# MoE2's gates of the second half and their sums kept in PSUM for VectorE, with low parts of the first half and of one tile of sums done by GpSimd

## The chip, the cores and the metric

The kernel runs on one core of a Trainium2 chip. The metric is the device time of one execution in microseconds (us), lower is better. The core has TensorE (PE; its weight loads are shown as PEld), VectorE (DVE), ScalarE (ACT), GpSimd (POOL) and SyncE (SP), which issues most of the loads and stores; each works through its own instructions in order and waits on semaphores for the others.

## The reference

```python
# q, k, v: (4, 8, 576, 64); 2304 tokens, model width 512
x = attention(q, k, v)          # softmax within chunks of 64 positions, 8 heads
p = domain_probs / sum(domain_probs)
y = sum(p[:, e] * (relu(x @ w1[e]) @ w2[e]) for e in range(4))     # MoE1, width 1024 for each e
h = y @ w_in                                                       # MoE2, (2304, 2048)
g = h * clip(h + 3, 0, 6) / 6                                      # the gates
out = g @ w_out                                                    # (2304, 512)
```

All is float32. The change concerns the last two lines.

## The kernel before

The 2304 tokens are worked on in three sets of 768. The program first runs MoE1 over the three sets (with the attention beside it), then MoE2 over the three sets; in MoE2 the width 2048 is cut into four groups of 512 (`g` = 0 to 3). One set and one group is a unit, so MoE2 has twelve units.

**Numbers.** Each float32 operand of TensorE is split into a high part (a rounded copy, made by ScalarE) and a low part (operand minus high part). A product is three matmuls: high by high, high by low, low by high (`HL`). `parts` makes the pair for gates and sums of gates: ScalarE writes the high part, then one TENSOR_TENSOR of VectorE or GpSimd writes the low part. TensorE's third matmul of each three needs the low part.

**The h part of a unit** (`h_pair`, two pairs, `pr_` = 0 and 1). Each pair is seven block products P1, P6, P7, P5, P2, P4, P3 of six matmuls of 384 columns, in four PSUM banks of tag `h` that are called a, b, c, d, with VectorE's additions `U`, `V`, `c22`, `c21`, `c12` between them (a Strassen form in Winograd's variant). `BACK` says where VectorE puts the results c22, c21, c12 of a pair: `p` in their own bank, `y` in a bank of tag `y`, `s` in SBUF. `gate` turns each of the four results of a pair into a gate: ScalarE's ACTIVATE makes the clipped part in an SBUF tile `t`, and VectorE's SCALAR_TENSOR_TENSOR (STT) multiplies it with the result in PSUM.

**The y part** (`y_sevens`, in the groups 0 to 2, nine units in all). The gates of a unit are four blocks A11, A12, A21, A22 of two tiles each (`k` = 0, 1; a tile is 128 x 384). Pair 0 gives A11 and A21, pair 1 gives A12 and A22. `gate_sums` makes S3 = A11 - A21, S1 = A21 + A22, S2 = S1 - A11 and S4 = A12 - S2, two tiles of each. TensorE then runs seven products in the order M1 (A11), M7 (S3), M2 (A12), M4 (A22), M5 (S1), M6 (S2), M3 (S4), each of 18 matmuls of 256 columns: three output tiles `j`, for each the six matmuls of `k` = 0 and then `k` = 1. M1 and M7, M2 and M4, M5 and M6 share banks, whose tags are in `YB`. In group 0 ScalarE copies the banks to totals in SBUF, in the groups 1 and 2 VectorE adds them (L1121). After group 2 `recombine` adds the totals to the output's blocks (L1135, two thirds on VectorE, a third on GpSimd). Group 3 is done plainly (`y_unit`, L1160, its additions L1203).

**PSUM** has eight banks here: four of tag `h`, three of `y`, one of `a`.

**GpSimd** also issues the loads of the split weights from scratch memory, in line with its additions: `wh` (L808, for the h part), `wy`, `wp` (L813) and `e` (L818, for the y part).

**The order.** All operations are handed to a planner (`Plan`) with an engine, an estimated cost (`dve`, `act`, `gps`, `mm`), a due time and what they need; it plays the program through with these costs and writes out a fixed order for each engine. So a new cost or due time can reorder an engine anywhere. `SLACK` and `LATER` are such numbers.

In the kernel before, all results of pair 1 are gated into SBUF tiles; the low parts of A11, A12, A22, S1 and S2 are VectorE's, those of S3 and S4 GpSimd's (`SLO`), and all sums are GpSimd's (L1056).

Of the kernel before, what the change touches and what calls it, by code (L numbers as in the profile page):

```python
# [22 lines left out]
SLACK = (7.93, 5.2, 6.37, 0.92)  # L23
# [218 lines left out]
def fused_kernel(ctx: ExitStack, tc: tile.TileContext, q, k, v, probs, w1, w2, win, wout, out):  # L242
# [80 lines left out]
    gps = lambda n: 0.03 + n * 0.0024  # L323
# [685 lines left out]
    def gate(u, f, z, src, bufs, after, due, n=N):  # L1009
# [9 lines left out]
        elif ph == 0:  # L1019
            hi = op("ACT", act(n), lambda: nc.scalar.activation(hi_(), src(), AF.Relu), due, after, [G], bufs)  # L1020
            lo = op("DVE", dve(n), lambda: nc.vector.scalar_tensor_tensor(out=lo_(), in0=src(), scalar=0.0, in1=raw(hi_()), op0=ALU.max, op1=ALU.subtract), due + 0.3, [hi, *after], (), [G, *bufs])  # L1021
        else:
            R = buf("t")
            r_ = lambda: R.t[:, :n]
            x = op("ACT", act(n), lambda: nc.scalar.activation(r_(), src(), AF.Relu, bias=half, scale=1.0 / 6.0), due, after, [R], bufs)  # L1025
            x = op("DVE", dve(n), lambda: nc.vector.scalar_tensor_tensor(out=r_(), in0=r_(), scalar=1.0, in1=src(), op0=ALU.min, op1=ALU.mult), due + 0.3, [x, *after], (), [R, *bufs])  # L1026
            if by_seven(u):
                name, k = A_OF[z, f % 2], f // 2
                raws[u, name, k] = (R, x)
                if name != "A21":  # L1030
# [55 lines left out]
    def y_sevens(u):  # L1086
# [6 lines left out]
        for q_, pair in enumerate(Y_PAIRS):  # L1093
            ps = [buf(YB[q_]) for _ in range(NJ)]
# [292 lines left out]
```

## Time and profile before

| | |
|---|---|
| median of 3 executions | 1214.36 us (1212.03 to 1214.58) |
| the profiled execution, and the span of its trace | 1214.51 us, 1212.7 us |
| busy: PE, DVE, POOL, ACT | 1176.5, 803.8, 675.9, 510.2 us |
| mean granted clock of TensorE | 0.994 |
| MoE2's first product starts at, span ends at | 815.28, 1212.7 us |

The span runs from the first to the last instruction; the remaining 1.8 us lie around it. Busy time is how long an engine had an instruction in it. Matmuls are pipelined and overlap in the trace, so the time that TensorE takes for a stretch of work is read from start to start, and the stalls from the idle time that the trace puts ahead of an instruction. The granted clock is 1.00 at 2.4 GHz and 0.50 at 1.2 GHz.

### The profile page before, as it was taken

The page shows a single profiled execution, that of the slowest core. Times are in us where ns is not written, and L with a number is a line of the kernel's source. Part 1 is how long each engine was busy: PE and PEld are TensorE (multiplying, and loading weights), DVE is VectorE, ACT ScalarE, POOL GpSimd, SP SyncE. Part 2 cuts the span into 40 slices and gives each one's busy share as a digit, 9 for nine tenths or more (in the row PEclk, how much of TensorE's full clock was granted, in tenths as well). Part 3 has the DMA queues.
Part 4 walks back from the last instruction along what each step waited for, and adds up shares of the span by engine and source line. Part 5 has one row for each costly group of instructions (what it writes and reads, how often), then busy time and mean ns, then how long its engine had stood idle before and what let it go on. Part 6 is the DMA issues. An engine that isn't in the chain of part 4 may idle for free.

```text
span 1212.7 us, 20698 instructions
## 1 busy us (share of the span) xinstructions
PE 1176.5 (97%) x7512; PEld 1077.7 (89%) x7512; DVE 803.8 (66%) x1414; ACT 510.2 (42%) x1205; POOL 675.9 (56%) x755
## 2 busy tenths in 40 slices
PE   8999999999999999999999999999999999899988
PEld 7898998888888999998998988989998999889987
DVE  5656555547466766567456566686889768976895
ACT  5755444433435343533332423245334453335322
POOL 3686665641464564737474756556663566526670
PEclk9999999999999999999999999999999999999999
DMA  9889877758789998777888988999965977577751
GB/s 241 290 305 321 276 263 252 277 202 265 213 261 316 279 334 265 261 245 246 266 287 277 323 254 274 351 295 257 303 218 194 262 256 236 169 239 243 229 171 53
DMA packets 153958, 311.27 MB, mean 257 GB/s; under 512 B 70528, under 2 KB 76928, under 8 KB 153856
## 3 DMA queue, kind: packets, MB, share of 16 engines
q0 software_dynamic: 48672, 172.51, 43.9%
q1 hardware_dynamic: 103440, 135.73, 34.9%
q10 hardware_dynamic: 1744, 1.70, 0.5%
q8 instruction: 59, 0.97, 0.3%
q14 instruction: 43, 0.35, 0.1%
HBM read 228.10 MB, written 81.79 MB: 256 GB/s over the span
## 4 chain that ended last, share of the span: by engine, by line
PE 81%; DVE 15%; ACT 2%; issue 2%; POOL 0%; DVEq 0%; POOLq 0%; ACTq 0%
PE h L937 37%; PE y L1160 33%; DVE gt L1050 4%; PE h L996 4%; PE y L1106 3%; DVE acc L1121 1%; DVE acc L1135 1%; DVE rh L1050 1%; PE h L1106 1%; DVE t L1026 1%; DVE xs L672 1%; DVE h L947 1%; DVE gt L1018 1%; DVE c L947 1%; PE a L545 1%
## 5 line engine op out<-in xcount | busy, mean ns | idle before, releaser
L937 PE MATMUL h<-x,wh 128*128 128x384 f32 x2772 | 494.1, 336 | 5.4 <-DVE c L947 5.2
L937 PEld LDWEIGHTS h<-x,wh 128*128 128x128 f32 x2772 | 482.0, 188 | 10.9 <-DVE c L947 7.8
L1160 PE MATMUL y<-wy,gt 128*128 128x512 f32 x1944 | 457.3, 393 | 4.7 <-DVE acc L1196 3.5
L1160 PEld LDWEIGHTS y<-wy,gt 128*128 128x128 f32 x1944 | 363.0, 188 | 82.5 <-DVE acc L1196 5.2
L808 POOL DMA_DIRECT2D wh<-k x190 | 104.7, 552 | 172.3 <-PE h L937 148.9
L1196 DVE SCALAR_TENSOR_TENSOR acc<-y,pn,acc 128x512 f32<-128x512 f32 x126 | 88.9, 750 | 129.9 <-PE y L1160 129.9
L813 POOL DMA_DIRECT2D wy<-k x112 | 61.9, 556 | 98.4 <-PE y L1160 84.6
L1020 ACT ACTIVATE gt<-h 128x384 fp32r<-128x384 f32 (+1 forms) x133 | 60.7, 484 | 112.4 <-DVE h L947 78.0
L1021 DVE SCALAR_TENSOR_TENSOR gt<-h,gt 128x384 fp32r<-128x384 f32 (+1 forms) x133 | 68.5, 539 | 43.3 <-ACT gt L1020 42.9
L947 DVE TENSOR_TENSOR c<-h,p 128x384 f32<-128x384 f32 x66 | 36.6, 555 | 85.1 <-PE h L937 70.5
L954 ACT COPY p<-h 128x384 f32<-128x384 f32 x66 | 31.4, 476 | 138.8 <-PE h L937 138.8
L1050 DVE TENSOR_TENSOR gt<-t,gt 128x384 fp32r<-128x384 f32 x96 | 86.5, 936 | 1.7 <-ACT gt L1048 0.5
L1056 POOL TENSOR_TENSOR t<-t 128x384 f32<-128x384 f32 x72 | 80.8, 1133 | 6.6 <-DVE gt L1050 4.9
L947 DVE TENSOR_TENSOR c<-h,c 128x384 f32<-128x384 f32 x120 | 66.4, 554 | 25.8 <-PE h L937 23.0
L1048 ACT CAST gt<-t 128x384 fp32r<-128x384 f32 x114 | 55.1, 513 | 55.6 <-POOL t L1056 28.7
L947 DVE TENSOR_TENSOR h<-h,c 128x384 f32<-128x384 f32 x111 | 62.5, 563 | 23.4 <-PE h L937 21.3
L873 POOL TENSOR_TENSOR w<-w,rh 128x512 f32<-128x512 f32 x28 | 37.4, 1336 | 52.4 <-issue 16.0
L728 POOL TENSOR_TENSOR wy<-t,wy 128x512 fp32r<-128x512 f32 x32 | 41.1, 1291 | 40.9 <-ACT wy L726 39.1
L1025 ACT ACTIVATE t<-h,half 128x384 f32<-128x384 f32 x72 | 39.6, 578 | 50.8 <-DVE h L947 38.3
L996 PE MATMUL h<-x,wh 128*128 128x384 f32 (+1 forms) x336 | 53.2, 314 | 0.5 <-DVE x L702 0.5
L996 PEld LDWEIGHTS h<-x,wh 128*128 128x128 f32 x336 | 51.4, 189 | 1.2 <-DVE x L702 0.7
L728 POOL TENSOR_TENSOR wp<-t,wp 128x512 fp32r<-128x512 f32 x32 | 43.8, 1368 | 13.4 <-ACT wp L726 13.0
(188 smaller groups left out, 1557.8 us busy)
## 6 DMA issues: line engine op xcount, KB each, us to landing
wh<-k POOLq DMA_DIRECT2D x190, 512.0 KB, 6.2
wy<-k POOLq DMA_DIRECT2D x112, 512.0 KB, 6.0
k<-wh SPq DMA_DIRECT2D x53, 512.0 KB, 3.7
k<-wp SPq DMA_DIRECT2D x53, 512.0 KB, 5.8
k<-wy SPq DMA_DIRECT2D x32, 512.0 KB, 3.2
wp<-k POOLq DMA_DIRECT2D x18, 512.0 KB, 5.8
t<-in_moe_w_dram SPq DMA_DIRECT2D x32, 256.0 KB, 4.7
w<-in_moe_w_in_dram SPq DMA_DIRECT2D x16, 512.0 KB, 6.0
```

What stands on the lines that cost most here:

```text
L728: return op(eng, gps(512) if eng == "POOL" else dve(512), lambda: e.tensor_tensor(out=view(b.t[:, 1]), in0=read(), in1=raw(view(b.t[:, 0]) ...
L808: wready[at_] = op("POOL", 0.6, lambda b=b, name=name: nc.gpsimd.dma_start(out=b.t, in_=kept[ph, g, name]), t - LEAD[0] + j, [stored[ph, g ...
L813: wready[key, "y", f] = op("POOL", 0.6, lambda b=b, f=f: nc.gpsimd.dma_start(out=b.t, in_=kept[ph, g, f]), t_y - LEAD[3] + n_, [stored[ph, ...
L937: nc.tensor.matmul(acc.t[:, :n], W.t[:, a, k_ * 256 + pr_ * P:k_ * 256 + (pr_ + 1) * P], X.t[:, b, k_, cs], start=new and first, stop=last ...
L947: add = lambda out, x, y: (lambda: nc.vector.tensor_tensor(out=out(), in0=x(), in1=y(), op=ALU.add))
L996: nc.tensor.matmul(ps.t[:, :m], Ws[k_ // 2].t[:, a, k_ % 2 * 256 + f % 2 * P:k_ % 2 * 256 + f % 2 * P + P], x if len(zs) == 2 else x[:, zs ...
L1020: hi = op("ACT", act(n), lambda: nc.scalar.activation(hi_(), src(), AF.Relu), due, after, [G], bufs)
L1021: lo = op("DVE", dve(n), lambda: nc.vector.scalar_tensor_tensor(out=lo_(), in0=src(), scalar=0.0, in1=raw(hi_()), op0=ALU.max, op1=ALU.sub ...
L1050: lo = op(eng, dve(N) if eng == "DVE" else gps(N), lambda: e.tensor_tensor(out=where()[:, 1], in0=r_(), in1=raw(where()[:, 0]), op=ALU.sub ...
L1056: return op("POOL", gps(N), lambda: nc.gpsimd.tensor_tensor(out=dst.t[:, :N], in0=x.t[:, :N], in1=y.t[:, :N], op=op_), due + m, after, new ...
L1160: nc.tensor.matmul(ps[j].t, G.t[:, a, o + j * P:o + (j + 1) * P], W.t[:, b, :], start=f == FO[0] and i == 0, stop=f == FO[-1] and i == len ...
L1196: fn = lambda: nc.vector.scalar_tensor_tensor(out=A.t, in0=ps.t, scalar=p, in1=A.t, op0=ALU.mult, op1=ALU.add)
```

## The change

Three tiles of pair 1 (`STAY`: both of A12, and `k` = 0 of A22) are gated in place: the STT writes to the PSUM bank of the result and not to the SBUF tile. Result c12 of pair 0 also stays in its own bank (`BACK`). What reads a gate in PSUM is VectorE's: the low parts of these three tiles, the sums S1, S2 of `k` = 0 and S4 of both `k`, the low parts of S1 and S4 of `k` = 0 (S1 of `k` = 0 is made in A22's bank, S4 of `k` = 0 in A12's, `S4_STAY`). GpSimd makes the low parts of A11 (both), A22 of `k` = 1, S1 of `k` = 1, S2 (both), S3 (both), S4 of `k` = 1, and the sums S3 (both), S1 and S2 of `k` = 1. Sums of `k` = 1 come first. `YB` now names a bank tag for each `j`. In a unit VectorE's low parts go from 10 to 5 and its sums from 0 to 4; GpSimd's low parts go from 4 to 9 and its sums from 8 to 4. TensorE's and ScalarE's instructions are as many as before.

```diff
-SLACK = (7.93, 5.2, 6.37, 0.92)
+SLACK = (7.97, 5.41, 6.27, 0.96)
...
-BACK = (("pys", "pps"), ("pys", "ppp"))
-SLO = ("DVE", "POOL", "DVE", "POOL")
+BACK = (("pys", "pps"), ("pyp", "ppp"))
 CO = ("DVE", "POOL", "DVE")
+STAY = (("A12", 0), ("A12", 1), ("A22", 0))
+S4_STAY = (0,)
 SUMS = 3.15
-YB = "yhyy"
-LATER = 0.35
+YB = ("yyy", "ahy", "yhh", "ahh")
+LATER = -1.0
...
-    gps = lambda n: 0.03 + n * 0.0024
+    gps = lambda n: 0.07 + n * 0.0024
...
             R = buf("t")
             r_ = lambda: R.t[:, :n]
+            name, k = (A_OF[z, f % 2], f // 2) if by_seven(u) else ("", 0)
+            stay = (name, k) in STAY
+            o_ = src if stay else r_
             x = op("ACT", act(n), lambda: nc.scalar.activation(r_(), src(), AF.Relu, bias=half, scale=1.0 / 6.0), due, after, [R], bufs)
-            x = op("DVE", dve(n), lambda: nc.vector.scalar_tensor_tensor(out=r_(), in0=r_(), scalar=1.0, in1=src(), op0=ALU.min, op1=ALU.mult), due + 0.3, [x, *after], (), [R, *bufs])
-            if by_seven(u):
-                name, k = A_OF[z, f % 2], f // 2
-                raws[u, name, k] = (R, x)
+            x = op("DVE", dve(n), lambda: nc.vector.scalar_tensor_tensor(out=o_(), in0=r_(), scalar=1.0, in1=src(), op0=ALU.min, op1=ALU.mult), due + 0.3, [x, *after], (), [R, *bufs])
+            if name:
+                raws[u, name, k] = (bufs[0] if stay else R, x)
                 if name != "A21":
-                    sevens[u, name, k] = parts("gt", R, [x], due + 0.6)
+                    sevens[u, name, k] = parts("gt", bufs[0] if stay else R, [x], due + 0.6, "DVE" if stay else "POOL")
+                rooms[u, name, k] = R
...
-        def sum_(dst, x, op_, y, after, m, new=()):
-            return op("POOL", gps(N), lambda: nc.gpsimd.tensor_tensor(out=dst.t[:, :N], in0=x.t[:, :N], in1=y.t[:, :N], op=op_), due + m, after, new, list({id(b): b for b in (dst, x, y)}.values()))
+        def sum_(eng, dst, x, op_, y, after, m, new=()):
+            e = nc.vector if eng == "DVE" else nc.gpsimd
+            return op(eng, dve(N) if eng == "DVE" else gps(N), lambda: e.tensor_tensor(out=dst.t[:, :N], in0=x.t[:, :N], in1=y.t[:, :N], op=op_), due + m, after, new, list({id(b): b for b in (dst, x, y)}.values()))
 
         def both(name, k, R, x, m):
             i = ("S1", "S3", "S2", "S4").index(name)
             tag = ("gt", "gt", "rh", "w64")[i]
-            share = (sevens[u, name, 0][0], 1) if tag == "rh" and k else None
-            sevens[u, name, k] = parts(tag, R, [x, *([sevens[u, name, 0][1]] if share else [])], due + m, SLO[i], share)
+            first = sevens.get((u, name, 1 - k))
+            share = (first[0], 1) if tag == "rh" and first else None
+            sevens[u, name, k] = parts(tag, R, [x, *([first[1]] if share else [])], due + m, "DVE" if name == "S1" and ("A22", k) in STAY or name == "S4" and k in S4_STAY else "POOL", share)
 
         if (u, "A22", 0) not in raws:
             for k in range(2):
                 (r11, x11), (r21, x21) = raws[u, "A11", k], raws[u, "A21", k]
                 s3 = buf("t")
-                both("S3", k, s3, sum_(s3, r11, ALU.subtract, r21, [x11, x21], 0, [s3]), 0.6)
+                both("S3", k, s3, sum_("POOL", s3, r11, ALU.subtract, r21, [x11, x21], 0, [s3]), 0.6)
             return
-        for k in range(2):
+        for k in (1, 0):
             (r11, x11), (r12, x12), (r21, x21), (r22, x22) = (raws[u, name, k] for name in ("A11", "A12", "A21", "A22"))
-            los = {name: sevens[u, name, k][1] for name in ("A11", "A12", "A22")}
-            s1 = sum_(r21, r21, ALU.add, r22, [x21, x22, sevens[u, "S3", k][1]], 0.1 * k)
-            both("S1", k, r21, s1, 0.8)
-            s2 = sum_(r11, r21, ALU.subtract, r11, [s1, los["A11"]], 2 + 0.1 * k)
-            both("S2", k, r11, s2, 2.8)
-            s4 = sum_(r12, r12, ALU.subtract, r11, [x12, s2, los["A12"]], 4 + 0.1 * k)
-            both("S4", k, r12, s4, 4.8)
-
-    sevens, raws, totals = {}, {}, {}
+            los = {name: sevens[u, name, k][1] for name in ("A11", "A22", "S3")}
+            m = 0.1 * (1 - k)
+            at = "DVE" if ("A22", k) in STAY else "POOL"
+
+            s1 = sum_(at, r22, r22, ALU.add, r21, [x21, x22, los["A22"]], m)
+            both("S1", k, r22, s1, 0.8 + m)
+            s2 = sum_(at, r11, r22, ALU.subtract, r11, [s1, los["A11"], los["S3"]], 1.2 + m)
+            both("S2", k, r11, s2, 2 + m)
+            R = r12 if k in S4_STAY else rooms[u, "A12", k]
+            s4 = sum_("DVE" if ("A12", k) in STAY else "POOL", R, r12, ALU.subtract, r11, [x12, s2], 3 + m)
+            both("S4", k, R, s4, 4 + m)
+
...
-            ps = [buf(YB[q_]) for _ in range(NJ)]
+            ps = [buf(YB[q_][j]) for j in range(NJ)]
```

**VectorE in the y part** of the second MoE2 unit (group 1 of the first set). `gt_`, `rh_`, `w64_` are high and low parts, `t_` SBUF tiles, `h_`, `y_`, `a_` PSUM banks, L1050 low parts, L1026 the STT, L1121 additions to totals. Before:

```order
L1026 SCALAR_TENSOR_TENSOR t_9449<-t_9449,h_9379 128x384
L1050 TENSOR_TENSOR gt_9470<-t_9439,gt_9470 128x384
L1050 TENSOR_TENSOR gt_9474<-t_9449,gt_9474 128x384
L1121 TENSOR_TENSOR acc_9111<-y_9430,acc_9111 128x512
L1121 TENSOR_TENSOR acc_9121<-y_9442,acc_9121 128x512
L1050 TENSOR_TENSOR gt_9500<-t_9348,gt_9500 128x384
L1050 TENSOR_TENSOR gt_9503<-t_9321,gt_9503 128x384
L1121 TENSOR_TENSOR acc_9143<-y_9454,acc_9143 128x512
L1050 TENSOR_TENSOR rh_9531<-t_9323,rh_9531 128x384
L1121 TENSOR_TENSOR acc_9173<-h_9493,acc_9173 128x512
L1121 TENSOR_TENSOR acc_9199<-h_9505,acc_9199 128x512
L1050 TENSOR_TENSOR rh_9531<-t_9345,rh_9531 128x384
```

In the change L1030 is the STT, L1054 low parts, L1061 sums, L1131 additions to totals:

```order
L1054 TENSOR_TENSOR gt_9436<-h_9337,gt_9436 128x384
L1030 SCALAR_TENSOR_TENSOR h_9376<-t_9447,h_9376 128x384
L1054 TENSOR_TENSOR gt_9457<-h_9365,gt_9457 128x384
L1131 TENSOR_TENSOR acc_9102<-y_9425,acc_9102 128x512
L1054 TENSOR_TENSOR gt_9469<-h_9376,gt_9469 128x384
L1131 TENSOR_TENSOR acc_9113<-y_9438,acc_9113 128x512
L1061 TENSOR_TENSOR h_9376<-h_9376,t_9348 128x384
L1131 TENSOR_TENSOR acc_9136<-y_9450,acc_9136 128x512
L1061 TENSOR_TENSOR t_9323<-h_9376,t_9323 128x384
L1061 TENSOR_TENSOR t_9432<-h_9365,t_9345 128x384
L1054 TENSOR_TENSOR gt_9518<-h_9376,gt_9518 128x384
L1061 TENSOR_TENSOR h_9337<-h_9337,t_9323 128x384
```

The rows with two SBUF tiles as inputs (`t_` with `gt_` or `rh_`) are gone: every row of the change reads a PSUM bank. Both low parts of S2 (`rh_`) have left VectorE, four sums have come, and the additions to totals now stand between them.

**GpSimd in the same y part**, from the low parts of S3 on. Before (L1056 sums, L1050 low parts, DMA rows are issues of loads):

```order
L1050 TENSOR_TENSOR gt_9390<-t_9376,gt_9390 128x384
L1050 TENSOR_TENSOR gt_9401<-t_9365,gt_9401 128x384
L808 DMA wh_9426<-k117_205 128x1024
L1056 TENSOR_TENSOR t_9321<-t_9321,t_9410 128x384
L808 DMA wh_9452<-k118_206 128x1024
L1056 TENSOR_TENSOR t_9345<-t_9321,t_9345 128x384
L808 DMA wh_9472<-k119_207 128x1024
L1056 TENSOR_TENSOR t_9348<-t_9348,t_9449 128x384
L1056 TENSOR_TENSOR t_9439<-t_9439,t_9345 128x384
L1056 TENSOR_TENSOR t_9323<-t_9348,t_9323 128x384
L813 DMA wy_9522<-k120_208 128x1024
L1056 TENSOR_TENSOR t_9412<-t_9412,t_9323 128x384
```

In the change (L1061 sums, L1054 low parts):

```order
L1054 TENSOR_TENSOR gt_9410<-t_9372,gt_9410 128x384
L1054 TENSOR_TENSOR gt_9422<-t_9403,gt_9422 128x384
L809 DMA wh_9460<-k117_205 128x1024
L1061 TENSOR_TENSOR t_9403<-t_9403,t_9321 128x384
L809 DMA wh_9485<-k118_206 128x1024
L1061 TENSOR_TENSOR t_9345<-t_9403,t_9345 128x384
L1054 TENSOR_TENSOR gt_9488<-t_9403,gt_9488 128x384
L809 DMA wh_9521<-k119_207 128x1024
L1054 TENSOR_TENSOR rh_9509<-t_9345,rh_9509 128x384
L814 DMA wy_9541<-k120_208 128x1024
L1054 TENSOR_TENSOR w64_9538<-t_9432,w64_9538 128x384
L1054 TENSOR_TENSOR rh_9509<-t_9323,rh_9509 128x384
```

Two sums (S1 and S2 of `k` = 1) stand where six did, and low parts of A22, S1 and S2 have come in; the low part of S2 of `k` = 0 (`rh_` from `t_9323`) is the last. The issues of loads are the same ones.

**VectorE in MoE1**, at the end of the second set's stretch, ahead of three additions L1196 to totals (L1206 in the change). Before:

```order
L702 TENSOR_TENSOR x7_65<-xs_4246,x7_65 128x768
L1018 TENSOR_TENSOR gt_6460<-c_6396,gt_6460 128x384
L870 TENSOR_SCALAR rh_6174<-t_6401 128x512
L702 TENSOR_TENSOR x7_65<-xs_4246,x7_65 128x768 x2
L672 TENSOR_TENSOR xs_4246<-xs_4246 128x2x384
L1196 SCALAR_TENSOR_TENSOR acc_3931<-y_6436,pn_79,acc_3931 128x512
L1196 SCALAR_TENSOR_TENSOR acc_3936<-y_6444,pn_79,acc_3936 128x512
L1196 SCALAR_TENSOR_TENSOR acc_3947<-y_6449,pn_79,acc_3947 128x512
```

In the change:

```order
L871 TENSOR_SCALAR rh_6174<-t_6401 128x512
L703 TENSOR_TENSOR x7_65<-xs_4246,x7_65 128x768
L1019 TENSOR_TENSOR gt_6463<-c_6396,gt_6463 128x384
L703 TENSOR_TENSOR x7_65<-xs_4246,x7_65 128x768
L673 TENSOR_TENSOR xs_4246<-xs_4246 128x2x384
L1206 SCALAR_TENSOR_TENSOR acc_3931<-y_6435,pn_79,acc_3931 128x512
L1206 SCALAR_TENSOR_TENSOR acc_3937<-y_6441,pn_79,acc_3937 128x512
L1206 SCALAR_TENSOR_TENSOR acc_3947<-y_6446,pn_79,acc_3947 128x512
```

Of the four wide operations on `xs` and `x7` (L702 and L672, in the change L703 and L673) that stand in these rows ahead of the additions, three are left; one L702 stands earlier in the list, and an L672 that stood there has moved behind the additions.

## Rows read from the trace of the kernel before

**Rows 1.** Waits of PE, 815 to 1213: who waited for whom, total, times, longest.

```profile
PE y L1106 <- DVE rh L1050: 10.9, 6, 2.2
PE h L937 <- DVE c L947: 5.2, 4, 1.9
PE h L1106 <- DVE gt L1050: 4.9, 8, 0.6
```

**Rows 2.** Timeline of PE in MoE2: start, us, instructions, idle before and its releaser.

```profile
815.28 12.67 PE L937 MATMUL h<-x,wh 128*128 128x384 f32 x72
...
830.96 4.47 PE L1106 MATMUL y<-wy,gt 128*128 128x256 f32 x36
...
840.30 2.30 PE L1106 MATMUL y<-wp,gt 128*128 128x256 f32 x18
...
846.76 14.72 PE L937 MATMUL h<-x,wh 128*128 128x384 f32 x84
861.32 4.47 PE L1106 MATMUL y<-wy,gt 128*128 128x256 f32 x36
...
913.28 5.37 PE L937 MATMUL h<-x,wh 128*128 128x384 f32 x30
...
929.88 8.36 PE L1160 MATMUL y<-wy,gt 128*128 128x512 f32 x36
...
946.73 14.75 PE L937 MATMUL h<-x,wh 128*128 128x384 f32 x84
...
1043.03 5.40 PE L937 MATMUL h<-x,wh 128*128 128x384 f32 x30
...
1061.86 8.36 PE L1160 MATMUL y<-wy,gt 128*128 128x512 f32 x36
...
1078.93 14.75 PE L937 MATMUL h<-x,wh 128*128 128x384 f32 x84
...
1176.18 5.37 PE L937 MATMUL h<-x,wh 128*128 128x384 f32 x30
...
1192.47 16.52 PE L1160 MATMUL y<-wy,gt 128*128 128x512 f32 x72
```

**Rows 3.** Timeline of DVE around the y part that starts at 861.32.

```profile
854.71 0.55 DVE L1050 TENSOR_TENSOR gt<-t,gt 128x384 fp32r<-128x384 f32 x1
...
859.88 1.09 DVE L1026 SCALAR_TENSOR_TENSOR t<-t,h 128x384 f32<-128x384 f32 x2 [0.92 <-ACT t L1025]
...
864.88 2.56 DVE L1050 TENSOR_TENSOR gt<-t,gt 128x384 fp32r<-128x384 f32 x2
```

**Rows 4.** Timeline of POOL in the same stretch.

```profile
856.08 2.33 POOL L1056 TENSOR_TENSOR t<-t 128x384 f32<-128x384 f32 x2
...
859.46 2.00 POOL L1050 TENSOR_TENSOR gt<-t,gt 128x384 fp32r<-128x384 f32 x2
```

**Rows 5.** Groups by line and shape, 815 to 1213: count, busy us, mean ns, idle before.

```profile
L1050 DVE TENSOR_TENSOR gt<-t,gt 128x384 fp32r<-128x384 f32 x96 | 86.5, 936 | 1.7 <-ACT gt L1048 0.5
L1056 POOL TENSOR_TENSOR t<-t 128x384 f32<-128x384 f32 x72 | 80.8, 1133 | 6.6 <-DVE gt L1050 4.9 <-DVE t L1026 0.9
...
L808 POOL DMA_DIRECT2D wh<-k x76 | 41.8, 551 | 86.0 <-PE h L937 86.0
...
L947 DVE TENSOR_TENSOR h<-h,c 128x384 f32<-128x384 f32 x48 | 27.1, 564 | 8.8 <-PE h L937 7.6
...
L1121 DVE TENSOR_TENSOR acc<-h,acc 128x512 f32<-128x512 f32 x18 | 11.7, 678 | 0.0
...
L672 DVE TENSOR_TENSOR xs<-xs 128x768 f32<-128x768 f32 x8 | 7.6, 955 | 0.0
```

**Rows 6.** Windows: busy us (count) of PE, PEld, DVE, ACT, POOL, granted clock, DMA.

```profile
908.50:911.90 3.40, 3.40 (x18) 3.40 (x18) 3.35 (x9) 0.00 (x0) 1.33 (x2) 0.50 0.70 231
1051.90:1055.20 3.30, 3.30 (x12) 3.30 (x11) 2.62 (x6) 2.02 (x4) 0.00 (x0) 0.50 0.00 0
```

**Rows 7.** Timeline of PE in MoE1: its longest stall there.

```profile
552.50 3.83 PE L1160 MATMUL y<-wy,gt 128*128 128x512 f32 x10 [1.83 <-DVE acc L1196]
```

More of the change, by code (lines that the diff above doesn't have):

```diff
@@ L1067, in gate_sums @@
                 s3 = buf("t")
-                both("S3", k, s3, sum_(s3, r11, ALU.subtract, r21, [x11, x21], 0, [s3]), 0.6)
+                both("S3", k, s3, sum_("POOL", s3, r11, ALU.subtract, r21, [x11, x21], 0, [s3]), 0.6)
             return
-        for k in range(2):
+        for k in (1, 0):
             (r11, x11), (r12, x12), (r21, x21), (r22, x22) = (raws[u, name, k] for name in ("A11", "A12", "A21", "A22"))
-            los = {name: sevens[u, name, k][1] for name in ("A11", "A12", "A22")}
-            s1 = sum_(r21, r21, ALU.add, r22, [x21, x22, sevens[u, "S3", k][1]], 0.1 * k)
-            both("S1", k, r21, s1, 0.8)
-            s2 = sum_(r11, r21, ALU.subtract, r11, [s1, los["A11"]], 2 + 0.1 * k)
-            both("S2", k, r11, s2, 2.8)
-            s4 = sum_(r12, r12, ALU.subtract, r11, [x12, s2, los["A12"]], 4 + 0.1 * k)
-            both("S4", k, r12, s4, 4.8)
-    sevens, raws, totals = {}, {}, {}
+            los = {name: sevens[u, name, k][1] for name in ("A11", "A22", "S3")}
[8 more added lines that the diff above has]
+            both("S4", k, R, s4, 4 + m)
+    sevens, raws, rooms, totals = {}, {}, {}, {}
     A_OF = {(0, 0): "A11", (0, 1): "A12", (1, 0): "A21", (1, 1): "A22"}
```

## The prediction

> **What bounds the kernel now.** TensorE is busy nearly everywhere, so what can be won is the time in which it stands. I read the views in this order: TensorE's waits, its timeline from start to start, the timelines of VectorE and GpSimd around one y part, then the groups by shape for prices. In MoE2, TensorE's waits are for VectorE alone [rows 1]: 10.9 us in 6 stalls for low parts of S2 (`rh`), 4.9 us in 8 for low parts of A12 (L1106 in `h` banks is M2), and 5.2 us for `c`, the sums U and V of an h part.
>
> The timeline gives the full loss [rows 2]. A clean h part takes 861.32 - 846.76 = 14.56 us. M5, M6 and M3 of the first unit ran clean: 54 matmuls in 846.76 - 840.30 = 6.46 us, 0.1196 us each, so a clean y part of 126 takes 15.07. From 830.96 to 1192.47 are 361.51 us. Taken off: eight clean h parts (116.48), the three h parts of the groups 3 (16.60 from 913.28, 18.83 from 1043.03, 16.29 from 1176.18: 51.72) and two plain y parts (929.88 to 946.73 and 1061.86 to 1078.93: 33.92). That leaves 159.39 us for nine y parts that need 135.6: **23.8 us lost**, 2.6 in each. Of it 10.9 + 4.9 are stalls. The rest is their aftermath, refilling and low clock: right after one of the longest stalls on S2, TensorE ran 3.4 us at a granted clock of 0.50, the level of 1.2 GHz [rows 6], which costs half of it, 1.7 us.
>
> Why VectorE is late stands in its timeline. A low part from two SBUF tiles takes 0.55 us alone (854.71) but two of them 2.56 at 864.88 [rows 3], while GpSimd was making sums; the mean over MoE2 is 0.936 [rows 5]. An STT that reads one SBUF tile and one PSUM bank kept 0.55 at 859.88 [rows 3] beside GpSimd's low parts, which kept 1.00 each from 859.46 [rows 4]. So two SBUF inputs meet GpSimd, and a PSUM input does not.
>
> **The change, walked through one y part.** T is the start of M1. Products start at T + 2.15 (M7), 4.31 (M2), 6.46 (M4), 8.61 (M5), 10.76 (M6) and 12.92 (M3); each needs the low part of `k` = 0 at its third matmul, 0.24 us later, and of `k` = 1 at its sixth.
>
> VectorE: c12 of pair 1 ends at about T + 0.8 in both kernels (TensorE's P3 ends at T + 0.2, plus 0.56). From there the order runs STT, low, STT, low, addition, low, addition, S1, addition, S2, S4, low of S1, S4. The trace has no row of these exact forms; between an STT's 0.55 and 0.564 for an addition into a bank [rows 5] I take 0.56, with 0.68 for additions to totals [rows 5]. Low parts of A12 are then ready by T + 3.1 (needed from 4.55, the second at 4.9), of A22 `k` = 0 by 4.3 (needed at 6.7), S1's by T + 0.8 + 9 x 0.56 + 3 x 0.68 = 7.9 (needed at 8.85), S4's by about 10.4 (needed at 13.2). S4 of `k` = 1, in the middle of this, needs GpSimd's S2, which by the next paragraph's prices is there at 4.9. So the A12 stalls go and no new one comes on this engine.
>
> GpSimd is now the long chain. Its second sum of S3 ended at 858.41 before [rows 4], T - 2.9; two low parts of A11 now stand ahead of it, one in time that was idle, so I take T - 2.4. Behind it come nine operations (two lows of S3, low of A22, S1, S2, low of S1, low of S2, low of S4, low of S2) and six issues of loads. At 1.03 (the pair's 1.00 [rows 4] and a little for starts after a pause) and 0.55 for an issue [rows 5], that is 9 x 1.03 + 6 x 0.55 = 12.6: the last low part lands at T + 10.2, and M6 needs it at 11.0. **Margin 0.8 us.** The first two must be there for M7 at 2.4: T - 2.4 + 2 x 0.55 + 2 x 1.03 = 0.8. The prices' other bound is 1.133, GpSimd's mean for sums while VectorE met it [rows 5]: then T + 11.1, and M6 waits 0.1. The loads behind need no early issue: they are for the next unit, 15 us on.
>
> The Trainium skill speaks against this part: "GPSIMD Engine Reference", section 4.1 "Engine selection", gives elementwise work on a tile to VectorE, with GpSimd about twice as slow for two inputs. The rows agree on the ratio (1.03 to 0.55). By the rule alone, five more low parts of 0.48 extra in nine units would add 21.6 us; by the rows they cost VectorE 0.94 in company and lie on neither engine's end, so the sum takes nothing for them.
>
> So the nine y parts give back **23.8 us**; bounds: 9.4, with a stall of 1.6 us in each (the first rival), and no more than all.
>
> The h part of the first unit lost 830.96 - 815.28 - 14.56 = 1.1 us [rows 2], the fourth of the stalls on `c`, where V stood behind three transposes on VectorE; in the new order one stands ahead of V: **-1.1**, bound 0.
>
> The h parts of the groups 3 lost 2.0, 4.3 and 1.7 us [rows 2], 8.0 in all, to `c` behind `recombine`, whose work is the same. Before, stalls in M6 gave VectorE time; now M6 and M3 run through, but VectorE no longer comes to its additions of M6 from a late low part of S2. I take a stall of 1.6 us, a little under the 1.9 of the second set [rows 1], and 0.15 for refilling in each, and the 1.7 of low clock once, as it came after that 1.9 [rows 6]: 5.2 + 1.7 = 6.9, so **-1.1**; bounds -2.8 (no low clock) and +2.3 (three times).
>
> MoE1 is reordered in small swaps. TensorE's longest stall there is 1.83 us at 552.50 [rows 7], for totals behind wide subtractions. One of these (0.955, [rows 5]) no longer stands ahead: **-1.0**. Bounds: the stall and its low clock gone, -3.5, or one more like it, +3.5.
>
> Sum: 23.8 + 1.1 + 1.1 + 1.0 = 27.0, from the profiled execution's 1214.5 (the median of the runs is 0.15 less): **1187.5 us**.
>
> **The rivals.**
>
> *GpSimd ends last.* Its chain has 0.8 us of margin. If VectorE's new forms still met it, an operation would take 1.16, the mean of the two sums at 856.08, or 1.30, what one of them took if the other took 1.03 [rows 4]. At 1.30 the chain ends 9 x 0.27 = 2.4 later, M6 stalls 1.6 in each y part, and 14.4 us stay: 1202. At 1.16 it stalls 0.4: 1191. Against it: the 1.00 us beside an STT. Any stall of this kind sits on M6, or on M7 if the S3 sums slip.
>
> *The wait only moves.* S2 of `k` = 0 now goes through four hands (VectorE S1, VectorE S2, ScalarE's high part, GpSimd's low part), and VectorE's additions to totals wait for TensorE in between. If it landed as late as before, the 10.9 us of [rows 1] stay with their aftermath and the 4.9 go: about 1206 too, whatever GpSimd's prices.
>
> *Banks are held too long, and it is slower.* Three of four `h` banks hold gates into the y part, M2 to M3 take what is left, and the next h part starts in banks that M6 and M3 filled. By the walk the A22 bank is free at T + 7.9 and wanted for M5's third tile at T + 10.0; the next P1 wants at T + 15.1 what VectorE adds by about T + 13. These 2.1 us are the point that decides: VectorE later than that by d costs d in each unit, and the kernel is slower than before from d = 3.0, where 27 us are eaten. At d = 4: 1214.5 - 27 + 36 = 1223. "PSUM — Partial Sum Buffer" of the Trainium skill, section "Summary: rules for kernel authors", advises to empty PSUM promptly because it is tight, and would expect this. No run here shows it yet; in the trace of before no wait for such a bank is among TensorE's waits [rows 1].
>
> *It does nothing there*, because VectorE meets GpSimd with one SBUF input too: 1214, against the 0.55 us at 859.88.
>
> **How the numbers follow.** The walk as told, with errors of some tenths a unit: 0.58 (1181 to 1193). GpSimd last or the wait moved: 0.28 (1191 to 1207). Banks: 0.08, half of it slower than before. Nothing: 0.03. Something in MoE1 that eats the gain: 0.03. The range 1181 to 1204 leaves out about 2 in 10. A difference of 0.2%, 2.4 us, is about what a measurement can tell: faster 0.90, same 0.04, slower 0.06.
>
> **What would show it.** Right: no stall of L1116 on `rh` or on M2; VectorE's low parts in the y part at 0.54 to 0.58; GpSimd's operations there near 1.03, the last one ending by T + 10.5; y parts of 15.1 us start to start; no 0.50 clock in a y part. Wrong: stalls on M6 released by GpSimd, VectorE's rows over 0.7, stalls at the first products of an h part released by additions to totals, or longer stalls on `c` in the groups 3. MoE2's start at other than 814 us is MoE1's doing.

## The result, and the profile after

| | before | after |
|---|---|---|
| median | 1212.0 us (6 runs, 1210.21 to 1214.58) | **1190.64 us** (6 runs, 1189.4 to 1193.41) |
| ratio, 95% interval | | **0.9822** [0.9805, 0.9839] |
| profiled execution, span | 1214.51, 1212.7 us | 1190.68, 1188.7 us |
| busy: PE, DVE, POOL, ACT | 1176.5, 803.8, 675.9, 510.2 us | 1169.8, 755.3, 674.9, 507.0 us |

VectorE is busy 48.5 us less, though it has only one operation a unit fewer (nine lows and sums for ten lows): on average each became shorter, 0.55 us and not 0.94 to 1.18. The waits of TensorE in MoE2 after the change, the whole list, to be read beside [rows 1]:

```profile
PE h L938 <- DVE c L948: 4.9, 3, 1.9
PE y L1170 <- DVE acc L1213: 0.6, 2, 0.4
```

The waits for `rh` and for `gt` in front of M2, 10.9 and 4.9 us before, are gone; those for `c` are left. The timeline of TensorE, the rows that answer to [rows 2]:

```profile
814.88 14.75 PE L938 MATMUL h<-x,wh 128*128 128x384 f32 x84
829.47 4.47 PE L1116 MATMUL y<-wy,gt 128*128 128x256 f32 x36
...
844.55 14.72 PE L938 MATMUL h<-x,wh 128*128 128x384 f32 x84
859.12 4.47 PE L1116 MATMUL y<-wy,gt 128*128 128x256 f32 x36
...
874.20 14.72 PE L938 MATMUL h<-x,wh 128*128 128x384 f32 x84
...
904.35 5.37 PE L938 MATMUL h<-x,wh 128*128 128x384 f32 x30
...
911.60 11.70 PE L938 MATMUL h<-x,wh 128*128 128x384 f32 x54 [1.88 <-DVE c L948]
923.14 8.36 PE L1170 MATMUL y<-wy,gt 128*128 128x512 f32 x36
...
1036.04 10.29 PE L938 MATMUL h<-x,wh 128*128 128x384 f32 x54 [1.52 <-DVE c L948]
...
1158.90 9.63 PE L938 MATMUL h<-x,wh 128*128 128x384 f32 x54 [1.52 <-DVE c L948]
```

Start to start, a y part takes 15.08 us (829.47 to 844.55, 859.12 to 874.20), the clean price; eight of nine do, and the third takes 15.59. Why the others are clean shows in VectorE's timeline in the y part that starts at T = 859.12, beside [rows 3], and in GpSimd's, beside [rows 4]:

```profile
860.25 0.55 DVE L1054 TENSOR_TENSOR gt<-h,gt 128x384 fp32r<-128x384 f32 x1
...
861.18 0.55 DVE L1054 TENSOR_TENSOR gt<-h,gt 128x384 fp32r<-128x384 f32 x1
...
866.02 0.55 DVE L1054 TENSOR_TENSOR gt<-h,gt 128x384 fp32r<-128x384 f32 x1
...
868.15 0.55 DVE L1054 TENSOR_TENSOR w<-h,w 128x384 fp32r<-128x384 f32 x1
```

```profile
867.10 1.03 POOL L1054 TENSOR_TENSOR w<-t,w 128x384 fp32r<-128x384 f32 x1
868.08 1.01 POOL L1054 TENSOR_TENSOR rh<-t,rh 128x384 fp32r<-128x384 f32 x1
```

VectorE's low at 868.15 runs beside GpSimd's at 868.08, and neither is lengthened. The same holds over MoE2: of VectorE's 81 lows and sums with an input in PSUM 80 overlap an operation of GpSimd, and none takes over 0.57 us; GpSimd's 117 lows and sums take 1.00 to 1.05. A12's lows end at T + 1.7 and T + 2.6, S1's at T + 7.5, GpSimd's last at T + 9.97.

In the third y part (T = 888.76) GpSimd's last low comes at T + 11.35, behind the 11.0 at which M6 needs it. GpSimd stood still for 1.33 us in front of the issue of a load, which by the profile waited for TensorE:

```profile
891.89 0.57 POOL L809 DMA_DIRECT2D wh<-k  x1 [1.33 <-PE y L1116]
...
899.10 1.02 POOL L1054 TENSOR_TENSOR rh<-t,rh 128x384 fp32r<-128x384 f32 x1
```

The groups by shape over MoE2, beside [rows 5]:

```profile
L1054 DVE TENSOR_TENSOR gt<-h,gt 128x384 fp32r<-128x384 f32 x36 | 19.9, 552 | 1.5 <-ACT gt L1052 1.3
L1061 DVE TENSOR_TENSOR h<-h,t 128x384 f32<-128x384 f32 x18 | 10.0, 558 | 0.1
...
L1061 POOL TENSOR_TENSOR t<-t 128x384 f32<-128x384 f32 x36 | 36.8, 1022 | 0.6
```

### The profile page after: what moved, and what is told of

It is laid out like the page before. It is cut to its first block, busy times and chain, and to the rows that moved or that the text cites. A ratio compares the mean times of both kernels' runs of the same rounds, so it can differ in the third digit from the quotient of the medians.

```text
span 1188.7 us, 20707 instructions
## 1 busy us (share of the span) xinstructions
PE 1169.8 (98%) x7512; PEld 1074.3 (90%) x7512; DVE 755.3 (64%) x1405; ACT 507.0 (43%) x1205; POOL 674.9 (57%) x764
## 4 chain that ended last, share of the span: by engine, by line
PE 87%; DVE 8%; DMA 2%; ACT 1%; issue 1%; SPq 0%; POOL 0%; DVEq 0%; ACTq 0%
PE h L938 37%; PE y L1170 33%; PE y L1116 5%; PE h L997 4%; PE h L1116 4%; PE a L1116 1%; DVE acc L1145 1%; DMA kr<-in_k_dram 1%; DVE gt L1019 1%; DMA k<-wp 1%; DVE xs L673 1%; PE h L555 1%; DVE c L948 0%; PE a L546 0%; PE y L465 0%
## 5 line engine op out<-in xcount | busy, mean ns | idle before, releaser
L938 PEld LDWEIGHTS h<-x,wh 128*128 128x128 f32 x2772 | 482.0, 188 | 10.2 <-DVE c L948 7.4
L1170 PEld LDWEIGHTS y<-wy,gt 128*128 128x128 f32 x1944 | 362.9, 188 | 83.3 <-DVE acc L1206 5.9
L1206 DVE SCALAR_TENSOR_TENSOR acc<-y,pn,acc 128x512 f32<-128x512 f32 x126 | 88.7, 749 | 125.6 <-PE y L1170 125.6
L948 DVE TENSOR_TENSOR h<-h,c 128x384 f32<-128x384 f32 x123 | 69.3, 563 | 30.1 <-PE h L938 28.7
L1054 POOL TENSOR_TENSOR gt<-t,gt 128x384 fp32r<-128x384 f32 x54 | 54.2, 1022 | 51.2 <-ACT gt L1052 51.1
L1029 ACT ACTIVATE t<-h,half 128x384 f32<-128x384 f32 x84 | 47.5, 581 | 78.6 <-DVE h L948 63.8
L948 DVE TENSOR_TENSOR c<-h,c 128x384 f32<-128x384 f32 x108 | 59.9, 555 | 25.9 <-PE h L938 23.3
L1116 PE MATMUL y<-wy,gt 128*128 128x256 f32 x432 | 56.1, 283 | 0.0
L1116 PEld LDWEIGHTS y<-wy,gt 128*128 128x128 f32 x432 | 54.1, 191 | 0.0
```

The costliest lines, as they stand in the source:

```text
L938: nc.tensor.matmul(acc.t[:, :n], W.t[:, a, k_ * 256 + pr_ * P:k_ * 256 + (pr_ + 1) * P], X.t[:, b, k_, cs], start=new and first, stop=last ...
L948: add = lambda out, x, y: (lambda: nc.vector.tensor_tensor(out=out(), in0=x(), in1=y(), op=ALU.add))
L1054: lo = op(eng, dve(N) if eng == "DVE" else gps(N), lambda: e.tensor_tensor(out=where()[:, 1], in0=r_(), in1=raw(where()[:, 0]), op=ALU.sub ...
L1116: nc.tensor.matmul(ps[j].t[:, 256 * i:256 * i + 256], Gs[k][2]()[:, a, j * P:(j + 1) * P], part(b)[:, 256 * k:256 * k + 256], start=k == 0 ...
L1170: nc.tensor.matmul(ps[j].t, G.t[:, a, o + j * P:o + (j + 1) * P], W.t[:, b, :], start=f == FO[0] and i == 0, stop=f == FO[-1] and i == len ...
L1206: fn = lambda: nc.vector.scalar_tensor_tensor(out=A.t, in0=ps.t, scalar=p, in1=A.t, op0=ALU.mult, op1=ALU.add)
```

## The experiments

The theory to be tested: VectorE's and GpSimd's operations lengthen one another only while both of VectorE's inputs lie in SBUF; gates in PSUM end that, and GpSimd's longer chain still ends 0.8 us early. The rivals: the new division of work is enough; the planner's numbers are enough; the bank tags don't matter. For each kernel the table has, from its profiled execution, start to start in TensorE's timeline (us; "g3" are the three h parts of the groups 3, added up; a wait at the very start of the next h part is not counted to a y part):

| kernel | median (runs) | ratio to before, interval | nine y parts | g3 h parts | MoE2 starts |
|---|---|---|---|---|---|
| before | 1212.0 (6) | | 159.3 | 51.7 | 815.3 |
| after | 1190.64 (6) | 0.9822 [0.9805, 0.9839] | 136.2 | 52.2 | 814.9 |
| after, again | 1189.34 (5) | 0.9795 [0.9776, 0.9813] | 136.2 | 50.8 | 814.4 |
| sbuf_gates | 1212.92 (10) | 0.9993 [0.9979, 1.0006] | 156.6 | 54.0 | 815.2 |
| lows_back | 1206.7 (10) | 0.9955 [0.9936, 0.9974] | 138.7 | 58.7 | 816.9 |
| old_banks | 1213.05 (10) | 0.9994 [0.998, 1.0008] | 160.4 | 51.6 | 813.8 |
| constants_only | 1207.54 (10) | 0.9973 [0.9948, 0.9998] | 154.1 | 50.3 | 812.5 |
| pool_plus1 | 1196.97 (5) | 0.9867 [0.985, 0.9885] | 139.7 | 52.8 | 814.8 |
| pool_plus2 | 1204.51 (6) | 0.9946 [0.993, 0.9961] | 149.2 | 52.7 | 812.8 |
| recombine_spread | 1189.21 (4) | 0.9807 [0.9791, 0.9824] | 136.2 | 51.2 | 814.7 |
| recombine_dve | 1193.73 (4) | 0.9825 [0.9808, 0.9843] | 136.2 | 52.0 | 814.9 |
| recombine_dve_spread | 1185.9 (4) | 0.977 [0.9748, 0.9791] | 136.2 | 47.2 | 815.1 |
| recombine_pool | 1191.49 (4) | 0.9815 [0.9802, 0.9829] | 136.2 | 53.1 | 814.7 |
| recombine_dve_late | 1186.55 (5) | 0.9797 [0.978, 0.9814] | 136.2 | 47.7 | 812.3 |

**sbuf_gates: the same division, gates in SBUF.**

```diff
-            o_ = src if stay else r_
+            o_ = r_
...
-                raws[u, name, k] = (bufs[0] if stay else R, x)
+                raws[u, name, k] = (R, x)
...
-                    sevens[u, name, k] = parts("gt", bufs[0] if stay else R, ...
+                    sevens[u, name, k] = parts("gt", R, ...
...
-            los = {name: sevens[u, name, k][1] for name in ("A11", "A22", "S3")}
+            los = {name: sevens[u, name, k][1] for name in ("A11", "A12", "A22", "S3")}
```

The last edit makes S4 wait for the low part of A12 (its use in S4's line is left out here), since S4 is now written over the gate that this low part reads.

> The changed kernel with one thing taken back: the three gates of pair 1 and the sums made over them lie in SBUF tiles again, while every operation stays on the engine that the change gave it (TensorE's and GpSimd's orders are the same, VectorE's nearly so). Theory (the gain is that VectorE's operations in the y part read one SBUF tile and so do not lengthen, nor lengthen GpSimd's): VectorE's lows and sums take about 0.94 us again and not 0.55, GpSimd's about 1.15 to 1.3 and not 1.03; S1's last low comes about 2 us later than T+7.45, behind the start of M5 at T+8.6, and GpSimd's last low about 1.5 us later than T+9.97, so each y part stalls 1.3 to 2 us: 1202 to 1208 us. Rival (the new division of the lows and sums over the two engines is enough): 1188 to 1193 us. Second rival (VectorE's operations with one SBUF input meet GpSimd as well, so nothing changes in their length): durations as in the changed kernel, 1188 to 1193 us.

All of the gain in time is gone, and with it 20.3 of the 23.1 us in the y parts; the median lies 5 us above the range expected. In the traces of the two kernels all four engines have the same operations in the same order in MoE2; only the place of the operands differs. Timelines of VectorE and, below, of GpSimd in the second y part of this kernel (T = 861.90):

```profile
863.03 1.09 DVE L1054 TENSOR_TENSOR gt<-t,gt 128x384 fp32r<-128x384 f32 x1
...
864.51 1.18 DVE L1054 TENSOR_TENSOR gt<-t,gt 128x384 fp32r<-128x384 f32 x1
...
866.21 3.53 DVE L1054 TENSOR_TENSOR gt<-t,gt 128x384 fp32r<-128x384 f32 x1
```

```profile
861.71 1.99 POOL L1054 TENSOR_TENSOR gt<-t,gt 128x384 fp32r<-128x384 f32 x2
...
864.23 1.03 POOL L1061 TENSOR_TENSOR t<-t 128x384 f32<-128x384 f32 x1
...
865.78 1.03 POOL L1061 TENSOR_TENSOR t<-t 128x384 f32<-128x384 f32 x1
866.76 1.02 POOL L1054 TENSOR_TENSOR gt<-t,gt 128x384 fp32r<-128x384 f32 x1
867.72 0.57 POOL L809 DMA_DIRECT2D wh<-k  x1
868.31 1.01 POOL L1054 TENSOR_TENSOR rh<-t,rh 128x384 fp32r<-128x384 f32 x1
```

VectorE's three lows end at 864.12, 865.69 and 869.74; GpSimd's operations before these ends finish at 863.70, 865.26 and 869.32. Each low ends 0.42 to 0.43 us after GpSimd is done: VectorE waits, and GpSimd keeps its 1.02. The Trainium skill has this in "SBUF — State Buffer", section "Who interferes with whom": a VectorE instruction with two SBUF inputs contends with a GpSimd instruction that reads SBUF, and the order of issue decides which of them blocks. The trace agrees (each of the three began during an operation of GpSimd) and goes beyond it: the third row also let two operations pass that began after it.

TensorE's stalls, 1.4 to 2.0 us in a y part, are of the size expected. What the expectation left out is the time lost around them, so that a y part loses 2.3, and 1.8 us more in the g3 h parts.

**lows_back: gates in PSUM, old share of lows.**

```diff
-..., due + 0.6, "DVE" if stay else "POOL")
+..., due + 0.6, "DVE")
...
-..., "DVE" if name == "S1" and ("A22", k) in STAY or name == "S4" ...
+..., "DVE" if name in ("S1", "S2") or name == "S4" and k in S4_STAY else "POOL", share)
```

> The changed kernel with the low parts of A11, of A22 and S1 with k = 1 and of S2 given back to VectorE; the gates in PSUM and the sums stay as the change has them, GpSimd keeps the lows of S3 and of S4 with k = 1 and its four sums. Theory (the gain needs the lows on GpSimd too, since VectorE's row of work ahead of S1 and S2 grows): two to five operations of 0.55 to 0.95 us more stand ahead of S1's and S2's last lows on VectorE, which then come at T+10 and later against M5 at T+8.6: 1.5 to 3 us of stall in a y part, 1203 to 1215 us. Rival (the gates in PSUM alone are enough): 1188 to 1193 us.

The median lies in the range that was expected, but not for the reason given: the theory put the loss into the y parts. They stay nearly clean, 138.7 us, so for them the gates in PSUM are nearly enough; of the 16 us lost they have 2.4. The two largest waits of TensorE in MoE2:

```profile
PE h L938 <- DVE c L948: 9.5, 4, 2.9
PE h L938 <- ACT tri L1129: 3.7, 1, 3.7
```

The lows that come back make VectorE late for U and V: the g3 h parts lose 6.5 us more than after, each with a stretch at granted clock 0.50, and the first h part waits again (15.68 us). So GpSimd's lows pay mostly in the h parts. (The wait for ScalarE is told below.)

**old_banks: the old bank tags.**

```diff
-YB = ("yyy", "ahy", "yhh", "ahh")
+YB = ("yyy", "hhh", "yyy", "yyy")
```

> The changed kernel with the old bank tags for the seven products (yyy, hhh, yyy, yyy). Theory (a gate in place holds its bank; the new tags keep TensorE from waiting for that): M2's second tile waits for the bank of A22 with k = 0, free after S1's low at T+7.45, its third for that of A12 with k = 1, about T+8.5, instead of starting at T+5.0 and T+5.8: about 3 us in each of nine y parts, 1212 to 1223 us, with waits h on gt or on VectorE's reads in front of M2. Rival (banks come free early enough in any tags): 1189 to 1193 us.

As the theory has it; the whole gain goes. TensorE at M2 of the second y part:

```profile
865.30 0.88 PE L1116 MATMUL h<-wy,gt 128*128 128x256 f32 x6
868.03 2.23 PE L1116 MATMUL h<-wy,gt 128*128 128x256 f32 x14 [1.85 <-DVE t L1061]
```

It waits for S4, the last reader of the bank of A12 with `k` = 1. Stalls of 0.6 to 3.2 us stand in all nine y parts; four were followed by a stretch at granted clock 0.50.

**constants_only: the old kernel with the planner's new numbers.**

```diff
-SLACK = (7.93, 5.2, 6.37, 0.92)
+SLACK = (7.97, 5.41, 6.27, 0.96)
-LATER = 0.35
+LATER = -1.0
-    gps = lambda n: 0.03 + n * 0.0024
+    gps = lambda n: 0.07 + n * 0.0024
```

> The kernel before with only the numbers of the planner changed (SLACK, LATER, GpSimd's estimated cost). Theory (these move MoE1's start by about a microsecond and nothing in the y parts): 1210 to 1214 us, y parts 17.5 us long as before. Rival (a new order of the same work gives a good share of the gain): under 1205 us.

Some 0.3% faster, more than I expected; the interval, up to 0.9998, barely excludes no change. The profiled execution, 1204.8 us, is one of the faster (1204.46 to 1217.62); its y parts take 154.1 and not 159.3 us. Waits in MoE2:

```profile
PE y L1106 <- DVE rh L1050: 10.3, 7, 2.1
...
PE h L1106 <- DVE gt L1050: 1.3, 2, 0.8
```

The new order alone takes most of the M2 stalls away, 4.9 us to 1.3; the waits for `rh` and their aftermath stay. So the planner's numbers alone have up to a fifth of the gain in the y parts (5.2 of 23.1 us), and reach it without any bank. What the change gives with the old numbers was not run.

**pool_plus1, pool_plus2: GpSimd's margin.** The low of S2 with `k` = 0 is written twice, or three times:

```diff
+        def low():
+            for _ in range(2 if tag == "rh" and i else 1):
+                x = e.tensor_tensor(out=where()[:, 1], in0=r_(), in1=raw(where()[:, 0]), op=ALU.subtract)
+            return x
...
```

> The changed kernel with GpSimd's last low of a y part (S2 with k = 0) written twice, the same values again: one operation of about 1.03 us more in each of nine y parts, all orders unchanged. Theory (GpSimd's chain ends 0.8 us ahead of M6): the last low ends at T+11.0, 0.2 to 0.5 us late, nine times: 1192 to 1195 us, and TensorE's wait in front of M6 is for rh from GpSimd. Rival (GpSimd's chain has more room than that, or none of its ends is ever waited for): 1190 to 1191 us. Rival (the second low also pushes the loads and sums behind it on GpSimd into TensorE's way): 1197 us and more.

> The same low written three times, so two operations of about 1.03 us more in each of nine y parts. Theory (0.8 us of room): 1.2 to 1.5 us late in a y part: 1201 to 1204 us. Rival (more room than 2 us): 1190 to 1192 us.

TensorE in one y part and GpSimd's lows of S2 there, first with one more operation, then with two:

```profile
959.25 4.47 PE L1120 MATMUL y<-wy,gt 128*128 128x256 f32 x36
...
974.54 2.76 PE L938 MATMUL h<-x,wh 128*128 128x384 f32 x15
```

```profile
968.20 2.10 POOL L1056 TENSOR_TENSOR rh<-t,rh 128x384 fp32r<-128x384 f32 x2
```

```profile
957.98 4.47 PE L1120 MATMUL y<-wy,gt 128*128 128x256 f32 x36
...
970.15 0.74 PE L1120 MATMUL y<-wp,rh 128*128 128x256 f32 x4 [1.01 <-POOL rh L1056]
...
974.33 2.94 PE L938 MATMUL h<-x,wh 128*128 128x384 f32 x16
```

```profile
966.92 3.18 POOL L1056 TENSOR_TENSOR rh<-t,rh 128x384 fp32r<-128x384 f32 x3
```

The y part takes 16.35 us (957.98 to 974.33) with two and 15.29 with one, against 15.08. GpSimd's last low ends at T + 12.12 and T + 11.05, against 9.97 in the changed kernel: 2.15 and 1.08 us later, of which 1.27 and 0.21 show. So 0.88 and 0.87 us were free, close to the margin of 0.8 in the prediction. The first and third y parts have less (15.81 and 16.96 with one more), and in the third the changed kernel lost 0.5 us. The median of pool_plus2 lies 0.5 us above its range; that of pool_plus1 lies 2 us above, and its profile has the ScalarE wait told below.

**What is left: `recombine` in front of U and V.** Five kernels tried to shorten this wait. The first puts the additions of `recombine` 8 us later (`due`) and changes VectorE's planned cost.

```diff
-            recombine(si, j, t + n_ * one - soon(u), CO[j])
+            recombine(si, j, t + n_ * one - soon(u) + 8.0, CO[j])
...
-            return op(eng, dve(256) if eng == "DVE" else gps(256), ...
+            return op(eng, 0.7 if eng == "DVE" else gps(256), ...
```

> The changed kernel with the additions of recombine due 8 us later and planned on VectorE at 0.70 us each (they take 0.41 to 0.96), so that in the h part of group 3 the first U stands behind nine of VectorE's fourteen and not behind all, V and c22 behind one more each. Theory (the three remaining stalls of 1.5 to 1.9 us in front of P2 are U, V and c22 queued behind recombine, and the stretch at half clock behind the first of them follows from it): the stalls go, 4.9 us, and the clock stretch with 1.7 us perhaps too: 1184 to 1187 us. Rival (the additions put behind U, V, c22 hold up gates or later additions, or GpSimd's third of recombine does, so the wait only moves): 1190 us or more.

The wait moved, as the rival said (the median, 1189.21, lies between the two forecasts): 2.2 us in each of two g3 h parts now wait for a gate and for later additions. In the next three kernels VectorE takes GpSimd's third too (`CO` all "DVE"); the same with `due` 8 us later at a planned cost of 0.36; and, the other way, all goes to GpSimd (`CO` all "POOL"):

> The changed kernel with GpSimd's third of recombine given to VectorE too, so twenty-one additions of VectorE in a row ahead of the group 3 h part and none of GpSimd beside them. Theory (a VectorE operation with both inputs in SBUF is long only while GpSimd works): each of the twenty-one takes 0.41 us, 0.33 from start to start, 7.0 us in all, against six of 0.87 and eight of 0.33 now, 7.9 us; the stall in front of P2 shrinks by 0.5 to 0.9 us in each of three h parts although VectorE does half as much again: 1187 to 1190 us. Rival (the lengthened ones are long by their own operands): twenty-one take 10 us and more, the stalls grow by 2 us each: 1196 us and more.

> As recombine_dve, and due 8 us later at a planned 0.36 us each, so that U stands behind fifteen of the twenty-one and V and c22 come between the rest. Theory (with no GpSimd beside them each addition in front of U, V or c22 costs 0.33 us and not 0.87): U no longer waits, and what is left of the three stalls is under 1 us each, with no clock stretch behind: 1184 to 1187 us. Rival (the additions placed later hold up the gates, as in recombine_spread, so the wait only moves): 1188 to 1191 us.

> The changed kernel with all of recombine on GpSimd. Theory (the three stalls in front of P2 are only VectorE's row of additions): VectorE has none of them, the three stalls of 4.9 us and the clock stretch of 1.7 us go: 1184 to 1186 us, if GpSimd's twenty-one additions (some 0.8 us each, about 17 us) end ahead of group 3's first additions of the y part. Rival (GpSimd's loads of wy and wh queue behind 17 us of additions and come late, or VectorE's lows beside them are long): TensorE waits for loads or for gt in group 3, 1190 us and more.

VectorE's additions of recombine of one form, min, median and max ns: first in the changed kernel, then in recombine_dve.

```profile
L1145 DVE TENSOR_TENSOR acc<-acc x12: 411/912/960, 900.2 to 1154.7; 128x256 f32<-128x256 f32 x12
```

```profile
L1145 DVE TENSOR_TENSOR acc<-acc x18: 415/419/421, 904.5 to 1158.0; 128x256 f32<-128x256 f32 x18
```

The theory holds at a second place: without GpSimd's additions beside them none of VectorE's, of any form, exceeds 0.422 us. The stalls did not shrink, though (2.07 each), and 1193.73 is above the range: seven more additions used up what the shorter ones gave. Spread (recombine_dve_spread), the remaining wait is this, against 4.9 us:

```profile
PE h L938 <- DVE t L1030: 2.0, 3, 0.7
```

The g3 h parts fall to 47.2 us. recombine_pool has no addition of VectorE ahead of U; instead, as its rival said, VectorE's lows of group 3, with both inputs in SBUF, meet GpSimd's 21 additions, and the next gates come late (TensorE waits 4.9 us for `t`, 1.3 for `c`). Two of these lows:

```profile
912.08 3.86 DVE L1054 TENSOR_TENSOR gt<-t,gt 128x384 fp32r<-128x384 f32 x2
```

The last one is recombine_dve_spread with `due` 14 us later:

> As recombine_dve_spread, with recombine due 14 us later and not 8, so that the first U of the second pair and its gates stand ahead of the last three additions instead of behind them. Theory (what was left there, 0.6 to 0.7 us in each group 3 h part in front of the second pair's products, was the gate queued behind these additions): 1 to 2 us less than recombine_dve_spread, 1183 to 1186 us, and no wait over 0.3 us in those h parts. Rival (that gate waits for ScalarE's clipped part and not for VectorE's queue): the waits of 0.6 to 0.7 us stay, 1184 to 1188 us.

It did not help: waits of 0.9 to 1.1 us for the gate, longer than before the shift, which neither the theory nor the rival had. Timed beside the changed kernel, recombine_dve_spread has a ratio of 0.977 [0.9748, 0.9791] to the kernel before where the changed one has 0.9795 [0.9776, 0.9813]. The profile shows where 3.6 us went (g3 from 50.8 to 47.2), but the intervals overlap, so it is not shown to be faster.

**Scatter.** In lows_back, pool_plus1, recombine_spread and recombine_dve TensorE waits 1.2 to 3.7 us for ScalarE's copy `tri` after the first y part. ScalarE in recombine_dve:

```profile
846.02 0.58 ACT L1129 COPY tri<-y 128x512 f32<-128x512 f32 x1 [6.43 <-DMA xs<-x2s]
```

By the profile it waited for a transfer of the MoE1 output; the four of them landed 18.5 to 22.9 us after their issue there, and 13.5 to 20.0 in the changed kernel. In recombine_spread and recombine_dve the order up to there is the changed kernel's, and the changed kernel's two profiles don't have the wait. Which run gets it is open.

## Why the prediction was right, step by step

Predicted 1187.5, measured 1190.64, in the range; between the profiled executions it is 23.8 us against 27.0. The mechanism and the largest term held; two small terms did not.

- **Nine y parts, -23.8:** measured 159.3 - 136.2 = 23.1. The walk held: VectorE's forms 0.55 to 0.57 (taken 0.56), GpSimd's last low T + 9.97 (T + 10.2), margin 0.87 to 0.88 (0.8). That the times came so near is in part luck: the walk added up whole durations, but operations in a row start closer together than they last (GpSimd's at 867.10 and 868.08 lie 0.98 apart at 1.03; VectorE's at 860.25 and 861.18, with one between them, 0.93 apart for two of 0.55), and GpSimd's row started 0.2 us later than taken. What it had wrong is that all units are alike, and that an issue of a load costs 0.55 us and never waits: in the third unit one waited 1.33 us, and 0.5 were lost.
- **First h part, -1.1:** 15.68 to 14.59, -1.1.
- **Groups 3, -1.1:** measured +0.45. Stalls of 4.9 and one low clock came as taken (4.8, once). Too small was the 0.15 for what follows a stall: it is 0.3 us in the third set and 0.9 in the second, as 17.02 and 16.36 us less 14.56 and the stall. The 0.66 between these two (10.29 and 9.63 for the same 54 matmuls, no low clock in either) are short waits late in the h part (from 1043.28 to 1045.29 matmuls start up to 0.39 us apart and not 0.17), where VectorE's additions stand behind wide operations on the next set's input; the third set has no next one. VectorE in the second set:

```profile
1043.53 0.95 DVE L673 TENSOR_TENSOR xs<-xs 128x768 f32<-128x768 f32 x1
1044.39 0.56 DVE L948 TENSOR_TENSOR h<-h,c 128x384 f32<-128x384 f32 x1
```

In the second profile of the same kernel the low clock is absent, and the term is -1.0: one profile can't settle it. The stretch at 912.5 in the first, then in the second profile (granted clock third from the end):

```profile
912.50:915.90 3.40, 3.40 (x13) 3.40 (x12) 1.97 (x5) 1.91 (x5) 0.00 (x0) 0.50 0.00 1
```

```profile
912.50:915.90 3.40, 3.40 (x21) 3.40 (x21) 3.31 (x8) 2.88 (x7) 1.04 (x3) 1.00 0.00 0
```

- **MoE1, -1.0:** -0.4. The step failed: the stall of [rows 7] is still there, at 1.96 us, with its low clock in this profile. One wide operation fewer did stand ahead. But an operation of GpSimd there now starts at 545.61 and not at 547.09, and a low of VectorE with both inputs in SBUF meets it and takes 1.67 us instead of 0.55: it ends 0.41 us after GpSimd's, the mechanism of the change itself at a place that the step had not looked at. constants_only has the same rows (1.67 us, a stall of 1.96), so they come with the planner's numbers. That the longer low made the stall is read from the rows; no run takes it away. TensorE, VectorE and GpSimd there:

```profile
552.58 3.83 PE L1170 MATMUL y<-wy,gt 128*128 128x512 f32 x11 [1.96 <-DVE acc L1206]
```

```profile
546.25 1.67 DVE L1019 TENSOR_TENSOR gt<-c,gt 128x384 fp32r<-128x384 f32 x1
```

```profile
545.61 1.90 POOL L874 TENSOR_TENSOR w<-w,rh 128x512 f32<-128x512 f32 x1 [6.52 <-ACT c L1017]
```

Twelve profiles of kernels with the changed one's order in MoE1 start MoE2 between 812.3 and 816.9, so whether the 0.4 are the change's can't be told: a term of 1 us there is below what one profile shows.
- **Rivals.** GpSimd ends last: true in one y part of nine, at 0.5 us, and 1 us more work makes it true in the others. The wait only moves: no, in the y parts. Banks held too long: true of the old tags, which eat all of the gain; the new ones are what keeps that rival out. It does nothing: sbuf_gates shows the opposite, the place of the gates is 20.3 of the 23.1 us in the y parts.

## What to carry to other kernels

Before moving work between VectorE and GpSimd, look at where VectorE's inputs lie: with both in SBUF most operations of VectorE that met GpSimd waited for GpSimd's to end. Neither division of the y part's work that was tried with SBUF gates cured that (the kernel before, sbuf_gates), while one input in PSUM did. A result left in PSUM holds its bank, so the change is worth only what the next user of that bank can spare: rotate the tags together with it. Price the slack of the engine that becomes the long chain by adding an operation to it, and look in its row for issues of loads that can wait.

## What was not expected of the hardware

A VectorE low of 0.55 us took 3.53 when GpSimd started its next operation at once (sbuf_gates, 866.21): it ended 0.42 us after the third, though 0.53 us of a load's issue lay between the second and the third. Of the 105 lows and sums of VectorE with two SBUF inputs in MoE2 of that kernel 64 kept under 0.7 us, 55 of them with no low or sum of GpSimd beside them. The other 41, all in the y parts, took 1.05 to 3.55, and every one ended 0.41 to 0.43 us after a GpSimd operation did.
